# A convolution front end on one Trainium2 core: the first batch's first convolution, one tile tap by tap and two tiles of output triples

## Chip, core and metric

The kernel runs on one core of a Trainium2 chip. The metric is the device time of one execution in microseconds (us). Three runs of the kernel before the change took 255.84, 256.33 and 256.61 us; the median is 256.33 us.

The core has five engines that work side by side and wait for each other through semaphores: TensorE (in the profile PE for its matmuls and PEld for its weight loads), VectorE (DVE), ScalarE (ACT), GpSimd (POOL) and SyncE (SP), which here issues all DMA transfers. Matmul results go to PSUM, eight banks of 512 float32 columns in each of 128 partitions.

## The reference

Two batches, 4,000 samples, 512 channels, 5 taps, 8 label steps, all in bfloat16:

```python
xp = jnp.pad(x, ((0,0),(pad,pad),(0,0)))
for i in range(K):
    h = h + jnp.einsum("btc,cd->btd", xp[:, i:i+T, :], w1[i])
h = _gelu(h)[:, ::2, :]            # 2,000 samples
# the same again with w2: f = _gelu(...)[:, ::2, :], 1,000 samples
fe = jnp.einsum("btd,de->bte", f, w_f)
ge = jnp.einsum("bud,de->bue", g, w_g)
j = jnp.tanh(fe[:, :, None, :] + ge[:, None, :, :])
return jnp.einsum("btud,dv->btuv", j, w_o)
```

Only every second output of a convolution is kept, so each is computed with stride 2. The output has 2 x 1000 x 8 x 512 values, 16 MB.

## The kernel before

**Layout.** Channels lie on the partitions, 4 slices of 128 of them (index k for inputs, m for outputs). Samples lie along the free dimension, split into phases: a buffer `xs[i]` holds phases 0 to 3 of x (sample 4j + phase at column j), a buffer `xp[i]` holds phases 0 to 5 (sample 6j + phase). One column j of `xs` gives a pair of outputs of the first convolution, one column of `xp` gives a triple.

**First convolution, first batch.** Its 1,002 pairs are three tiles (`tiles`): two of 252 columns out of `xs[0]` and one of 498 out of `xs[1]`. A pair is computed by filter products: seven matmul groups (named a0, a1, a2, a3, b1, b2, b3 in `xf`, `shift` and `weight`) in place of the ten that two outputs of five taps need. Each group is four matmuls (one for each k). They need sums and differences of phases, which VectorE (`xf`) and ScalarE (`shift`) write to `xt` or in place, and sums of taps, written to `w1_t` by `w1sums` and `w1sum13`. After the matmuls `post` or `unit` adds the parts, and a gelu on ScalarE writes `hT[0]`. In the first tile, output slice m = 0 is computed tap by tap (`direct`): ten groups of four matmuls of 252 columns, with five for each output of the pair; m = 1 to 3 use the filter products.

**Second batch and second convolution.** The second batch's first convolution (out of `xp[2]`, then `xp[0]`) and both batches' second convolution (out of `hT`) run as four `Triple` tiles of 334 columns. A triple takes nine products (t0, t1, t2, tm, ti, s0, s1, sm, si) where three outputs of five taps need fifteen. Its operands are written by `Triple.step` into a work buffer `row[0]` or `row[1]` or in place. Its tap sums come from `w1part` (into `w1_x`, `w1_t`, and in place) and `w2part`. One output slice of a tile is a `Unit` with the parts s1 to s5: s1 has the product t2 and a copy of it on ScalarE, s2 tm and sm, s3 t1 and s1 and two sums on VectorE, s4 t0 and s0, s5 ti and si; three gelus write the outputs. A loop over the units interleaves s1, s3, s5, s2, s4 of neighbouring units, and puts other work (transforms of the next tile, tap sums, loads) at numbered slots (`when`, `steps`).

**The start.** The first 256 columns of `xs[0]` come by two plain loads `xr` of 128 partitions with 4 samples each (`load_xr`, 512 KB a load), transposed on TensorE and copied from PSUM by VectorE (phases 0 and 2) and ScalarE (phases 1 and 3). All other samples come by transposing DMA (`load_x` for four phases, `load_x6` for six). SP issues, in this order: two `xr`, the five taps of w1 (each after the third transfer before it has landed), eight transposes into `xs`, six into `xp[2]`; later (`load_rest`) six into `xp[0]`, four small ones, the five taps of w2 and g.

**Order.** Every operation is recorded with what it reads and writes and a cost; `schedule` then fixes an order for each engine by list scheduling: TensorE, GpSimd and SP take the first recorded operation that is ready, VectorE and ScalarE the one that is due earliest. The order is fixed when the kernel is built; the chip's engines follow it and wait where something is late. Operations recorded while `pl.pin` is true keep the recorded order; it is set to False in the first convolution.

**The rest.** Products with w_f and w_g, tanh on ScalarE, and the last product with w_o (`Plain` tiles and tiles of seven products, `Seven`) follow to the end of the span. Their code is not changed, apart from places of scratch buffers.

Lines in the profile are lines of the kernel before; most operations are recorded in helpers: 412 memset, 415 tensor_tensor, 420 activation, 428 matmul, 447 a weight load, 452 `xr`, 460 and 467 transposing loads, 503 the transposes on TensorE, 510 their copies, 577 scalar_tensor_tensor.

The functions as they stand before the change:

Of the kernel before, what the change touches and what calls it, by code (L numbers as in the profile page):

```python
# [7 lines left out]
ACT = mybir.ActivationFunctionType  # L8
# [59 lines left out]
class Plan:  # L68
# [88 lines left out]
    def schedule(self, pred):  # L157
# [19 lines left out]
        free = {e: 0.0 for e in ("pe", "act", "dve", "pool", "sp")}  # L177
# [124 lines left out]
def bass_standalone__seq2seq_rnn_t_joint__speech_kernel(  # L302
# [25 lines left out]
    NA, NB = 252, 504  # L328
# [8 lines left out]
    WHOLE = 4  # L337

    with ExitStack() as es:
# [23 lines left out]
        c_off = cur[0]  # L363
        cs = [at(f"cs{i}", [NT], FP32) for i in range(2)]
        ty = [at(f"ty{i}", [2, 256], FP32) for i in range(3)]
        s_off = cur[0]
        ws = [at(f"ws{i}", [NK, P * (2 if i == 2 else 1)], FP32) for i in range(3)]
        ssum = [at(f"ssum{i}", [NK, P], FP32) for i in range(2)]
# [6 lines left out]
        sd = [Buf(nc, f"sd{i}", [3, 336], FP32, o) for i, o in enumerate((c_off, c_off + 4096, s_off + 4096))]  # L375
        assert sd[1].end <= ty[2].end and sd[2].end <= ws[2].end
        xp = {i: Buf(nc, f"xp{i}", [6, NK, 352], BF16, xs[i].end - xs[i].bytes) for i in (0, 2)}
        assert all(xp[i].end <= xs[i].end for i in xp)
        w1_x = Buf(nc, "w1_x", [3, NK, D], BF16, wf_sb.end - wf_sb.bytes)
# [15 lines left out]
        homes = [xt_off + 8192 + i * 2048 for i in range(4)] + [v.end - v.bytes for v in ssum + ws[:2]]  # L395
# [48 lines left out]
        memset(xs[1][:, :, NT:NT + 3])  # L444
# [3 lines left out]

        def load_xr(rt):
            dst = xr[rt][:].map(lambda a: a.rearrange("p r k c -> p (r k c)"))  # L450
            src = x[0, 4 * P * rt:4 * P * (rt + 1), :].rearrange("(p r) c -> p (r c)", r=4)
            return pl.dma("sp", lambda e: e.dma_start(dst.ap, src), (), (dst,))

        def load_x(s, ph, lo, hi):

            b, half = s // 2, s % 2
            i0 = half * NB + lo - 16
            dst = xs[s % 3][ph, :, lo:hi]
            src = x[b, 4 * i0 + ph:4 * (i0 + hi - lo - 1) + ph + 1:4, :]
            pl.dma("sp", lambda e: e.dma_start_transpose(out=dst.ap, in_=src), (), (dst,), nbytes=(hi - lo) * 2 * D, rate=185e3)  # L460

        def load_x6(i, b, ph, j0, col):

            r0 = b * T + 6 * j0 + ph
            dst = xp[i][ph, :, col:col + 336]
            src = x.rearrange("b t d -> (b t) d")[r0:r0 + 6 * 335 + 1:6, :]
            pl.dma("sp", lambda e: e.dma_start_transpose(out=dst.ap, in_=src), (), (dst,), nbytes=336 * 2 * D, rate=185e3)
# [4 lines left out]
        def load_w1(i, after=None):  # L472
            o = load_w("sp", w1_sb[i], w1[i].rearrange("(k c) d -> c k d", c=P))
            if after is not None:
                o.after.append(after.idx)
            return o

        came.append(load_w1(0))
        for i in (1, 3, 4, 2):
            came.append(load_w1(i, came[-3]))  # L480
        for ph in (2, 3, 1, 0):
            load_x(0, ph, 272, 528)
        for ph in (2, 3, 1, 0):
            load_x(1, ph, 0, 512)
        for ph in (4, 0, 2, 1, 3, 5):
            load_x6(2, 1, ph, 0, 16)

        def warm_mm(n):
            o, z, zz = ps.cols(3 * NT, NT), zero[0:P], zero[:]
            for _ in range(n):  # L490
                mm(o, [(z, zz)], True, True)

        warm_mm(NWARM)
        psb = ps.h[:, :].bitcast(BF16)
        for pp in range(2):
            for rt in range(2):
                bk = 4 + 2 * pp + rt
                pv = View(psb[:, bk * 1024:(bk + 1) * 1024].rearrange("p (r k c) -> p r k c", r=2, k=NK), np.array([bk]), True)

                def fn(e, rt=rt, pp=pp, pv=pv):  # L500
                    for r in range(2):
                        for k in range(NK):
                            ins = e.transpose(pv.ap[:, r, k, :], xr[rt].h[:, 2 * r + pp, k, :], ident.h[:, :])
                    return ins
                pl.op("pe", fn, (xr[rt][:], ident[:]), (pv,), 0.8)
                o = xs[0][pp::2, :, 16 + rt * P:16 + (rt + 1) * P]
                if pp:
# [3 lines left out]


        def shift(src, off, dst, c0, n, which):

            r, d, kind = {"a0": (2, -1, 0), "a3": (0, 1, 2), "b1": (3, -1, 3)}[which]
            act(dst[kind, :, c0:c0 + n], src[r, :, off + d:off + d + n], ACT.Copy)

        def xf(src, off, dst, c0, n, which, keep=False):


            ph = lambda r: src[r, :, off:off + n]
            o = lambda kind: dst[kind, :, c0:c0 + n]
            h = NT // 2
            if which == "a0" and keep:
                tt("dve", o(0), src[2, :, off - 1:off - 1 + n], ph(2), sub)
            elif which == "b3" and keep:
                tt("dve", dst[0, :, h:h + n], ph(3), ph(1), sub)
            elif which == "a2" and keep:
                tt("dve", dst[1, :, h:h + n], ph(2), ph(0), sub)
            elif which == "a0":  # L530
                tt("dve", o(0), o(0), ph(2), sub)
            elif which == "a3":
                tt("dve", o(2), o(2), ph(0), sub)
            elif which == "b1":
                tt("dve", o(3), o(3), ph(1), sub)
            elif which == "b3":
                tt("dve", ph(3), ph(3), ph(1), sub)
            elif which == "a1":
                tt("dve", o(1), ph(0), ph(2), add)
            elif which == "a2":  # L540
                tt("dve", ph(2), ph(2), ph(0), sub)

        def operand(src, off, dst, c0, n, which, k, keep=False):
            if keep and which in ("b3", "a2"):
                return dst[("b3", "a2").index(which), k, NT // 2:NT // 2 + n]
            if which in ("a0", "a1", "a3", "b1"):
                return dst[{"a0": 0, "a1": 1, "a3": 2, "b1": 3}[which], k, c0:c0 + n]
            r = {"b3": 3, "b2": 1, "a2": 2}[which]
            return src[r, k, off:off + n]

        def weight(which, k, m):
            sl = slice(m * P, (m + 1) * P)
            taps = {"a0": 0, "b1": 1, "b3": 3, "a3": 4}
            if which in taps:
                return w1_sb[taps[which], k, sl]
            return w1_t[{"a2": 0, "b2": 1, "a1": 2}[which], k, sl]

        def w1sum13():
            v = w1_t[1]
            tt("dve", v, w1_sb[1], w1_sb[3], add)  # L560
            act(v, v, ACT.Copy, scale=2.0)

        def w1sums(m, part):


            nm = 2 if m == 2 else 1
            sl = slice(m * P, (m + nm) * P)
            s = ws[m][:]
            if part == "s":
                tt("dve", s, w1_sb[0, :, sl], w1_sb[4, :, sl], add)  # L570
            elif part == "+":
                tt("dve", w1_t[2, :, sl], s, w1_sb[2, :, sl], add)
            else:
                tt("dve", w1_t[0, :, sl], s, w1_sb[2, :, sl], sub)
# [6 lines left out]
        def w2part(m, part):  # L581
            sl = slice(m * P, (m + 1) * P)
            w = lambda i: w2_sb[i, :, sl]
            t, v, u = ssum[0][:], ssum[1][:], ws[0][:]
# [12 lines left out]

        def w1part(m, part):
            sl = slice(m * P, (m + 1) * P)
            w = lambda i: w1_sb[i, :, sl]  # L600
            pl.hold = calm
            v, u = ssum[0][:], ssum[1][:]
            if part == "s":
                s = ws[m][:] if m < 2 else ws[2][:, (m - 2) * P:(m - 1) * P]
                tt("dve", v, s, w(2), sub)
# [3 lines left out]
                act(w1_x[1, :, sl], u, ACT.Copy, scale=1.0 / 3.0)  # L609
                tt("dve", w(2), w(1), w(3), add)  # L610
                tt("dve", w1_x[2, :, sl], w(1), w(3), sub)
            else:
                act(w(1), w(1), ACT.Copy, scale=2.0)
            pl.hold = []

        banks = list(range(8))
        ends = []

        def finish(keep=0):
            while len(ends) > keep:  # L620
                ends.pop(0)()

        class Tile_:
            def __init__(self, b, src, dst, c0, i0, n, keep=False):
                self.b, self.i0, self.n, self.keep = b, i0, n, keep
# [710 lines left out]
```

## Time and profile before

| | us |
|---|---|
| median of three runs (255.84 to 256.61) | 256.33 |
| the profiled execution, its own time | 256.88 |
| its span, first to last instruction | 255.1 |
| TensorE busy | 248.3 (97%) |
| VectorE busy | 221.4 (87%) |
| ScalarE busy | 209.3 (82%) |
| GpSimd busy | 106.4 (42%) |

The profile is of one execution. Busy time is the time in which an engine had at least one instruction in work. Matmuls are pipelined and their ends are modelled, so a length of 0.27 us for one of them is not its cost; the distance between starts is. The granted TensorE clock was 1.00 of full speed from the start to 230 us and 0.99 after it. In the lists a row has the start in us, the length in us, the engine, the line, the operation, output<-inputs with buffer numbers left out, the shape, and how many instructions were merged into the row. Rows of waits have the waiting engine and what it waited for, then the total in us, how often, and the longest.

### The profile page before, as it was taken

The numbers are of one execution on the slowest core, as the hardware profiler recorded it, in microseconds if no ns is written. First come the engines' busy times: TensorE is split into PE (matmuls) and PEld (weight loads), VectorE is DVE, ScalarE is ACT, GpSimd is POOL, SyncE is SP. The second block draws the span as 40 slices with busy tenths as digits, with TensorE's granted clock in tenths as the row PEclk, the third lists the DMA queues.
The fourth block names the chain that finished last, engine by engine and source line by source line (L and its number), as shares of the span: only waits on it lengthen the run. The fifth ranks groups of instructions, "written<-read, shape, count | busy, mean of one in ns | idle before, by whom it ended". The sixth has DMA issues, their size and how long they took to land.

```text
span 255.1 us, 5158 instructions
## 1 busy us (share of the span) xinstructions
PE 248.3 (97%) x1898; PEld 182.1 (71%) x1898; DVE 221.4 (87%) x359; ACT 209.3 (82%) x333; POOL 106.4 (42%) x108
## 2 busy tenths in 40 slices
PE   8899999998999999999999999999999999999995
PEld 3899954444666666667557888877778888778873
DVE  0999799999999999993346888899899999999892
ACT  2666695769997867985499999999999999998663
POOL 1000000000000000000708899698998999689940
PEclk9999999999999999999999999999999999999999
DMA  6999999979000016000001322423254436644548
GB/s 230 312 180 212 165 187 208 164 149 335 4 0 0 3 37 211 3 0 3 1 0 42 125 82 85 137 86 110 84 166 147 137 101 197 206 142 150 178 151 269
DMA packets 56006, 31.87 MB, mean 125 GB/s; under 512 B 32926, under 2 KB 55726, under 8 KB 55982
## 3 DMA queue, kind: packets, MB, share of 16 engines
q1 hardware_dynamic: 55982, 31.55, 46.2%
q8 instruction: 15, 0.25, 0.4%
q14 instruction: 9, 0.07, 0.1%
HBM read 7.87 MB, written 16.38 MB: 95 GB/s over the span
## 4 chain that ended last, share of the span: by engine, by line
PE 71%; DVE 11%; SPq 6%; DMA 6%; issue 3%; ACT 1%; ACTq 0%; DVEq 0%
PE acc L428 71%; SPq L460 6%; DMA xs<-in_x_dram 3%; DMA w_sb<-in_w_dram 2%; DVE acc L577 2%; DVE ssum L577 2%; DVE row L415 2%; DMA xr<-in_x_dram 1%; DVE xp L415 1%; DVE xt L415 1%; DVE ty L415 1%; ACT sn L1061 1%; DVE ty L577 1%; DVE ssum L415 1%; DVE og L415 0%
## 5 line engine op out<-in xcount | busy, mean ns | idle before, releaser
L415 DVE TENSOR_TENSOR og<-acc,sn 128x512 bf16<-128x512 f32 x87 | 56.9, 681 | 4.0 <-PE acc L428 3.1
L420 ACT ACTIVATE jT<-feT,geT 128x1000 bf16<-128x1000 f32 (+6 forms) x56 | 51.7, 974 | 0.5 <-DVE feT L945 0.4
L428 PE MATMUL acc<-tw,ss 128*128 128x256 f16 x348 | 48.0, 273 | 0.0
L1124 POOL TENSOR_TENSOR ss<-jT 128x512 f16<-128x512 bf16 x28 | 33.8, 1219 | 12.9 <-ACT jT L420 10.2
L428 PEld LDWEIGHTS acc<-tw,ss 128*128 128x128 f16 x348 | 33.5, 98 | 7.3 <-DVE sn L1062 0.3
L1061 ACT ACTIVATE sn<-acc 128x512 f32<-128x512 f32 x52 | 31.4, 618 | 3.5 <-PE acc L428 2.9
L412 POOL MEMSET hT<- 128x8 bf16 (+2 forms) x6 | 0.7, 146 | 75.8 <-ACT hT L420 70.4
L428 PE MATMUL acc<-wo_sb,jT 128*128 128x256 bf16 (+1 forms) x192 | 31.7, 290 | 0.0
L428 PE MATMUL acc<-row,w_sb 128*128 128x334 bf16 x160 | 29.0, 305 | 1.2 <-DVE acc L577 1.2
L420 ACT ACTIVATE jX<-feT,geT 128x1000 bf16<-128x1000 f32 (+4 forms) x28 | 25.0, 931 | 0.0
L428 PE MATMUL acc<-xt,w_sb 128*128 128x252 bf16 (+1 forms) x144 | 23.0, 305 | 0.0
L428 PEld LDWEIGHTS acc<-wo_sb,jT 128*128 128x128 bf16 x192 | 18.8, 98 | 5.7
L1124 POOL TENSOR_TENSOR ss<-jX 128x512 f16<-128x512 bf16 x18 | 20.8, 1174 | 1.2 <-ACT jX L420 0.7
L428 PEld LDWEIGHTS acc<-row,w_sb 128*128 128x128 bf16 x160 | 15.4, 97 | 8.0 <-DVE acc L577 1.5
L1062 DVE COPY sn<-acc 128x512 f32<-128x512 f32 x25 | 16.9, 682 | 2.4 <-PE acc L428 2.3
L428 PEld LDWEIGHTS acc<-xt,w_sb 128*128 128x128 bf16 x144 | 14.1, 98 | 6.0
L428 PE MATMUL acc<-wo_sb,ss 128*128 128x256 bf16 x116 | 17.9, 273 | 0.0
L428 PE MATMUL acc<-hT,w_t 128*128 128x334 bf16 x96 | 17.6, 305 | 0.0
L428 PE MATMUL acc<-xp,w_sb 128*128 128x334 bf16 x96 | 17.2, 304 | 0.0
L1124 POOL TENSOR_TENSOR ss<-ss,jT 128x512 f16<-128x512 f16 x14 | 16.5, 1182 | 0.7 <-PE acc L428 0.4
L1124 POOL TENSOR_TENSOR ss<-jT,ss 128x512 f16<-128x512 bf16 x14 | 16.6, 1188 | 0.3
L420 ACT ACTIVATE xt<-xs 128x1008 bf16<-128x1008 bf16 (+1 forms) x8 | 10.6, 1351 | 7.1 <-DMA xs<-in_x_dram 7.1
(109 smaller groups left out, 535.6 us busy)
## 6 DMA issues: line engine op xcount, KB each, us to landing
out_dram<-og SPq DMA_DIRECT2D x44, 256.0 KB, 2.3
w_sb<-in_w_dram SPq DMA_DIRECT2D x10, 512.0 KB, 5.4
out_dram<-og SPq DMA_DIRECT2D x14, 128.0 KB, 2.7
xr<-in_x_dram SPq DMA_DIRECT2D x2, 512.0 KB, 3.8
out_dram<-ost SPq DMA_DIRECT2D x7, 128.0 KB, 2.0
wf_sb<-in_w_f_dram SPq DMA_DIRECT2D x1, 512.0 KB, 3.8
wg_sb<-in_w_g_dram SPq DMA_DIRECT2D x1, 512.0 KB, 4.9
wo_sb<-in_w_o_dram SPq DMA_DIRECT2D x1, 512.0 KB, 5.9
```

Source lines behind the costliest of these rows:

```text
L412: pl.op("pool", lambda e: e.memset(v.ap, 0.0), (), (v,))
L415: pl.op(eng, lambda e: e.tensor_tensor(out=o.ap, in0=a.ap, in1=b.ap, op=op), (a, b), (o,), 0.02 + 2.14e-3 * o.ap.free_size() if eng == "po ...
L420: pl.op("act", lambda e: e.activation(o.ap, i.ap, func, scale=scale, bias=0.0 if bias is None else bias.ap), rd, (o,), o.ap.free_size() * ...
L428: ins = e.matmul(o.ap, lhsT=l.ap, rhs=r.ap, start=start and n == 0, stop=stop and n == len(pairs) - 1, skip_group_check=not check)
L460: pl.dma("sp", lambda e: e.dma_start_transpose(out=dst.ap, in_=src), (), (dst,), nbytes=(hi - lo) * 2 * D, rate=185e3)
L577: pl.op(eng, lambda e: e.scalar_tensor_tensor(out=o.ap, in0=a.ap, scalar=f, in1=b.ap, op0=ALU.mult, op1=add), (a, b), (o,), vec_cost(o, (a ...
L1061: pl.flex({"act": (lambda e: e.activation(o.ap, v.ap, ACT.Copy), 0.05 + n * 0.833e-3), "dve": (lambda e: e.tensor_copy(out=o.ap, in_=v.ap) ...
L1062: "dve": (lambda e: e.tensor_copy(out=o.ap, in_=v.ap), 0.065 + n * 1.04e-3)}, (v,), (o,))
L1124: fn = lambda e, o=S[i], x=x, y=y, op=op: e.tensor_tensor(out=o.ap, in0=x.ap, in1=y.ap, op=op)
```

## The change

The first batch's first convolution is cut differently:

- The first tile has 216 pairs (`NA`) and is computed tap by tap for all four output slices. Both outputs of a pair go through one matmul of 432 columns: `both` makes one operand out of two stretches of 216 columns, a fixed step apart. The order is tap 0, 4, 2, 1, 3, and for each tap all four m. Banks 0 to 3 hold the results, and one gelu for each m reads them.
- The other pairs are two `Triple` tiles of 262 columns (`N3`), out of new six-phase buffers: `xq[0]` in the place of `xs[1]`, `xq[1]` in the place of `w2_sb`. The classes and helpers of the filter products (`Tile_`, `xf`, `shift`, `operand`, `weight`, `w1sums`, `w1sum13`) are gone.
- All tap sums of w1 come from `w1part`, which no longer writes w1 in place.
- `Triple` has a number of columns of its own, keeps sm and ti in other rows, and its steps are split finer (d0 to d2, r0 to r2).
- There are 24 units in place of 16, and the slots move. PSUM banks 0 to 2 are kept for second accumulators (`later`) until the second convolution's last unit.
- The second `xr` load has 90 partitions. The load order changes; the five taps of w2 move from `load_rest` to a new `load_w2` at slot 9 (after the second triple tile).
- The planner's DMA rate and start offsets change.

```diff
-    def dma(self, eng, fn, reads=(), writes=(), sem=None, nbytes=524288, rate=345e3):
+    def dma(self, eng, fn, reads=(), writes=(), sem=None, nbytes=524288, rate=320e3):
-        free = {e: 0.0 for e in ("pe", "act", "dve", "pool", "sp")}
+        free = {e: 0.75 for e in ("pe", "act", "dve", "pool", "sp")}
-    NA, NB = 252, 504
+    NA, N3 = 216, 262
...
+        xq = [Buf(nc, f"xq{i}", [6, NK, 288], BF16, v.end - v.bytes) for i, v in enumerate((xs[1], w2_sb))]
...
+        NR = (P, NA + 2 - P)
...
+        def load_xq(i, ph):
+            load_x6(xq[i], 0, ph, 2 * NA // 3 + i * N3 - 2, 0, -(-(N3 + 3 - i) // 16) * 16)
+        for kind, i in (('w', 0), ('w', 4), ('w', 2), ('w', 1), ('w', 3), ('x', 4), ('x', 0), ('x', 2), ('x', 1), ('x', 3), ('x', 5)):
...
+        for ph in (4, 0, 2, 1, 3, 5):
+            load_xq(1, ph)
...
-                if pp:
+                if rt:
                     act(o, pv, ACT.Copy)
...
             if part == "s":
+                t, v, u = ssum[4][:], ssum[m % 2][:], ssum[2 + m % 2][:]
+                if m in w13:
+                    n = slice(m * P, w13[m] * P)
+                    act(w1_t[1, :, n], w1_sb[1, :, n], ACT.Copy, scale=2.0)
+                    tt("dve", w1_t[0, :, n], w1_sb[1, :, n], w1_sb[3, :, n], add)
+                    tt("dve", w1_x[2, :, n], w1_sb[1, :, n], w1_sb[3, :, n], sub)
+                tt("dve", t, w(0), w(4), add)
                 stt("dve", u, w(4), 4.0, w(0))
                 stt("dve", u, w(2), 2.0, u)
+                act(w1_x[1, :, sl], u, ACT.Copy, scale=1.0 / 3.0)
+                tt("dve", v, t, w(2), sub)
                 act(w1_x[0, :, sl], v, ACT.Copy, scale=1.0 / 3.0)
+                tt("dve", w1_t[2, :, sl], t, w(2), add)
...
+        banks, later = [4, 5, 6, 7, 3], [0, 1, 2]
...
+        trip = [Triple(xq[0], 2, row[0], wa, to_h(0, j3, N3), N3), Triple(xq[1], 2, row[1], wa, to_h(0, j3 + N3 // 2, N3), N3),
+                Triple(xp[2], 16, row[0], wa, to_h(1, 0)), Triple(xp[0], 4, row[1], wa, to_h(1, NT3 // 2)),
...
+        memset(xq[1][0:4, :, 1 + N3:4 + N3])
+        memset(xq[1][4:6, :, N3:4 + N3])
+        taps = (0, 4, 2, 1, 3)
+        def both(i, k):
+            a, b = (xs[0][r, k, 16 + d:16 + d + NA] for r, d in tap_at[i])
+            lo, hi = a.ap, b.ap
+            ap = bass.AP(tensor=lo.tensor, offset=lo.offset, ap=[list(lo.ap[0]), [hi.offset - lo.offset, 2], [1, NA]])
+            return View(ap, np.union1d(a.cells, b.cells), False)
+        def direct(i, m):
+            mm(ps.cols(m * NT, 2 * NA), [(w1_sb[i, k, m * P:(m + 1) * P], both(i, k)) for k in range(NK)],
+               i == taps[0], i == taps[-1])
+        for i in taps:
+            for m in range(NK):
+                direct(i, m)
...
-        STEPS = ("2d", "r", "t2", "t1", "prev", "s1", "tm", "si", "sm", "next", "t0", "s0", "ti")
+        STEPS = ("d2", "d1", "d0", "r2", "r1", "t2", "tm", "sm", "r0", "t1", "s1", "prev", "s0", "next", "t0", "ti", "si")
...
+        w1part(0, "s")
+        for w in STEPS:
+            trip[0].step(w)
+        for m in range(1, NK):
+            when((0, 0, 1)[m - 1], lambda m=m: w1part(m, "s"))
+        when(17, load_late, lambda: tail_zero(1))
+        for i in range(1, len(trip) - 1):
+            steps(4 * i - 4 + 1, i, 0, 3)
+            steps(4 * i - 4 + 1, i, 3, 6)
+            steps(4 * i - 4 + 2, i, 6, 9)
+            steps(4 * i - 4 + 3, i, 9, 17)
+        when(0, load_rest)
+        when(9, load_w2)
...
-        nu = 13
+        nu = 21
```

More of the change, by code (lines that the diff above doesn't have):

```diff
@@ L362, in bass_standalone__seq2seq_rnn_t_joint__speech_kernel @@
         assert hT[0].end <= h_off + 16384 and xr[1].end <= cur[0]
[L363 to L368, printed above, removed]
+        sd = [at(f"sd{i}", [3, 336], FP32) for i in range(3)]
+        ssum = [at(f"ssum{i}", [NK, P], FP32) for i in range(5)]
         geT = at("geT", [NK * BU], FP32)
@@ L394, in bass_standalone__seq2seq_rnn_t_joint__speech_kernel @@
         assert fT[0].end <= xt_off and ost[-1].end <= h_off + hT[0].bytes
-        homes = [xt_off + 8192 + i * 2048 for i in range(4)] + [v.end - v.bytes for v in ssum + ws[:2]]
+        homes = [xt_off + 8192 + i * 2048 for i in range(4)] + [v.end - v.bytes for v in ssum[:4]]
         sn = [at(f"sn{i}", [NT], FP32, o) for i, o in enumerate(homes)]
@@ L454, in load_x @@
[L454 to L462, printed above, removed]
+            n = NR[rt]
+            dst = xr[rt].rows(0, n).map(lambda a: a.rearrange("p r k c -> p (r k c)"))
@@ L469, in bass_standalone__seq2seq_rnn_t_joint__speech_kernel, with load_w1 @@
         came = [load_xr(rt) for rt in range(2)]
         act(warm[0:1], warm[1:2], ACT.Gelu_apprx_tanh)
-        def load_w1(i, after=None):
+        def load_w1(i):
             o = load_w("sp", w1_sb[i], w1[i].rearrange("(k c) d -> c k d", c=P))
[L474 to L482, printed above, removed]
@@ L483, in bass_standalone__seq2seq_rnn_t_joint__speech_kernel @@
-        for ph in (2, 3, 1, 0):
-            load_x(1, ph, 0, 512)
+            if len(came) > 2:
+                o.after.append(came[-3].idx)
+            came.append(o)
+        def load_xq(i, ph):
+            load_x6(xq[i], 0, ph, 2 * NA // 3 + i * N3 - 2, 0, -(-(N3 + 3 - i) // 16) * 16)
+        for kind, i in (('w', 0), ('w', 4), ('w', 2), ('w', 1), ('w', 3), ('x', 4), ('x', 0), ('x', 2), ('x', 1), ('x', 3), ('x', 5)):
+            if kind == "w":
+                load_w1(i)
+            else:
+                load_xq(0, i)
@@ L543, in operand @@
[L543 to L556, printed above, removed]
@@ L727, in step @@
+                if which[0] == "d":
+                    i = int(which[1])
+                    act(r(i, n=E), z(2 * i - 2, 0, E) if i else z(4, -1, E), ACT.Copy, scale=2.0)
+                elif which[0] == "r":
+                    i = int(which[1])
+                    tt("dve", r(i, n=E), r(i, n=E), z(2 * i, 0, E), sub)
                 elif which == "next":
-                    act(r(3), r(0, 1), ACT.Copy)
+                    act(z(3), r(0, 1), ACT.Copy)
                 elif which == "prev":
@@ L988, in tail_zero @@
             memset(v)
-        tile = tiles[2]
-        calm = [pl.ops[-1].idx]
-        for m in range(NK):
-            vec = [[lambda: trip[0].step("2d"), lambda: w1part(0, "s")],
-                   [lambda: trip[0].step("r"), lambda: trip[0].step("t2"), lambda: trip[0].step("prev"),
-                    lambda: trip[0].step("t1"), lambda: w1part(1, "s")],
-                   [lambda: trip[0].step("s1"), lambda: trip[0].step("tm"), lambda: trip[0].step("si"),
-                    lambda: trip[0].step("sm"), lambda: w1part(0, "d"), lambda: w1part(2, "s")],
-                   [lambda: trip[0].step("next"), lambda: trip[0].step("t0"), lambda: trip[0].step("s0"),
-                    lambda: trip[0].step("ti"), lambda: w1part(1, "d"), lambda: w1part(3, "s")]][m]
-            tile.unit(m, vec)
-            if m == 0:
-                load_rest()
+        joint = []
         units = [Unit(t, m) for t in trip for m in range(NK)]
-        STEPS = ("2d", "r", "t2", "t1", "prev", "s1", "tm", "si", "sm", "next", "t0", "s0", "ti")
+        STEPS = ("d2", "d1", "d0", "r2", "r1", "t2", "tm", "sm", "r0", "t1", "s1", "prev", "s0", "next", "t0", "ti", "si")
         fixed = {}
```

322 lines of the change are left out of this document (57 added, 265 removed).

## The prediction, made before the changed kernel was run

> **What bounds the kernel now.** I read first the busy shares and the slices, then who TensorE waited for, then its rows and its timeline in the first 64 us.
>
> ```profile
> PE 248.3 (97%) x1898; PEld 182.1 (71%) x1898; DVE 221.4 (87%) x359; ACT 209.3 (82%) x333; POOL 106.4 (42%) x108
> ...
> DVE  0999799999999999993346888899899999999892
> ```
>
> TensorE works 248.3 of 255.1 us, and VectorE is full until about 109 us. Who TensorE waited for:
>
> ```profile
> PE acc L428 <- DVE zero L435: 1.2, 1, 1.2
> PE acc L428 <- DVE acc L577: 1.2, 1, 1.2
> PE acc L428 <- DVE xs L510: 0.7, 1, 0.7
> PE acc L428 <- DVE og L415: 0.4, 1, 0.4
> PE acc L428 <- DVE w_x L415: 0.3, 1, 0.3
> ```
>
> Only 3.8 us, all but 0.4 before 63.3 us; from there to 251 us TensorE is dense. So time gained on TensorE in the first convolution should reach the end nearly one for one, and a new wait there costs as much. The page's busy times per group overlap; what a matmul costs is read from the starts of groups that follow each other (columns: start, length, engine, line, operation):
>
> ```profile
> 32.56 0.59 PE L428 MATMUL acc<-xs,w_t 128*128 128x252 bf16 x4
> 32.99 0.59 PE L428 MATMUL acc<-xt,w_sb 128*128 128x252 bf16 x4
> 33.42 1.00 PE L428 MATMUL acc<-xs,w_t 128*128 128x498 bf16 x4
> 34.26 1.00 PE L428 MATMUL acc<-xt,w_t 128*128 128x498 bf16 x4
> ```
>
> Four of 252 columns take 0.43 us, four of 498 take 0.84: columns at 2.4 per ns plus 2.5 ns, 107.5 and 210 ns each.
>
> **TensorE's own work.** Removed from the first batch: the first tile has 40 matmuls tap by tap and 84 in filter products, the second 112, all of 252 columns; the third 112 of 498. 236 x 0.1075 + 112 x 0.210 = 48.89 us. Added: 5 taps x 4 slices x 4 outputs = 80 matmuls of 432 columns (182.5 ns by the same slope), and 2 tiles x 9 products x 16 = 288 of 262 columns (111.7 ns): 14.60 + 32.16 = 46.76. That saves 2.13 us. The 432 columns lie in two stretches of one operand, which no row shows; the nearest has three stretches:
>
> ```profile
> 123.24 1.01 PE L428 MATMUL acc<-fT,wf_sb 128*128 128x501 bf16 x4
> ```
>
> Its three starts cover 1.01 less one length of 0.376, 211 ns each, as 501 plain columns would: I take no penalty; 4 ns each, the most I can read into these digits, would be 0.3 us.
>
> A rule speaks against the exchange of many narrow matmuls for fewer wide and more narrow ones. The Trainium skill ("TensorE: Matmul & The Clock Gate", section Back-to-back issue gap) gives for streams of weight load and matmul 81 ns at 128 columns and 131 ns at 512, so that width is cheap and the count of matmuls matters. An estimate between its two figures is 37.3 us before and 38.0 after, a loss of 0.7. The trace does not agree: 498 columns take 210 ns, where that estimate has 129.
>
> **The start.** The first convolution matmul starts at 8.04 us, and the wait is put down to VectorE; the load of tap 0 is what came last:
>
> ```profile
> 1.65 0.43 SPq L447 DMA_DIRECT2D w_sb<-in_w_dram  x1
> ...
> w_sb<-in_w_dram SPq DMA_DIRECT2D x1, 512.0 KB, 6.3
> ```
>
> 1.65 + 6.3 = 7.95. The shorter sample block takes 152 KB (38 of 128 rows) from ahead of it, at the 312 GB/s of that slice 0.5 us. The copies of phases 0 and 2 now run on two engines at once (VectorE 6.1 to 6.75, ScalarE about 6.5 to 7.3) and stay ahead. I take a start at 7.55 and a gain of 0.45; bounds 0 and 0.5. Tap 4, loaded second, then lands at 9.43 - 0.45 = 9.0.
>
> **Stalls that go.** The 0.3 and the 1.17 us at 55 and 62 us are first triple products waiting for a VectorE busy without a gap. In the new kernel VectorE loses, from the first batch, 18 tile transforms, the old weight sums and all combining after the tiles: by starts some 47 us before; after it 24 weight sums (14.4), 24 transforms (14.6), the sums of 8 units (5.4) and copies (1.4), some 36. By the second batch it has lead, so I count 1.47 us gained there. What is late next lies earlier: the new hand-over.
>
> **The hand-over to triples.** The tap-by-tap tile needs only samples and taps, ends at 7.55 + 14.60 = 22.15 and covers the preparation. Two things must be ready then.
>
> First the samples, issued on SP behind the weights. Four 256-row transposes took from issue to landing:
>
> ```profile
> xs<-in_x_dram SPq DMA_TRANSPOSE x1, 7.2
> xs<-in_x_dram SPq DMA_TRANSPOSE x1, 6.4
> xs<-in_x_dram SPq DMA_TRANSPOSE x1, 4.8
> xs<-in_x_dram SPq DMA_TRANSPOSE x1, 3.9
> ```
>
> With their issues at 9.86, 11.51, 14.56 and 16.81 they landed at 17.1, 17.9, 19.4 and 20.7, later rows at about 5.3 ns each (8 landed 3,072 rows by 31.95). With 272 rows each, 0.45 us earlier, the phases 4, 0, 2, 1, 3, 5 land near 16.7, 17.7, 19.2, 20.5, 22.0, 23.4. The first product wants phase 2 doubled on ScalarE (1.04 us for 1008 columns, row xt<-xs) and two VectorE steps: 19.2 + 1.1 + 0.1 + 2 x 0.61 + 0.1 = 21.7, just under 22.15. The second tile's set ends near 32.5; its edge memsets on GpSimd wait for whole phase groups, and the double, subtract, subtract behind the last makes its first operand ready near 35, when it is due at 34.7 and some 3.5 us of the first tile's products can still go first.
>
> Second, VectorE. Its cost, too, is from starts:
>
> ```profile
> 55.80 0.68 DVE L415 TENSOR_TENSOR ssum<-ws,w_sb 128x512 f32<-128x512 f32 x1
> 56.40 0.42 DVE L415 TENSOR_TENSOR w_sb<-w_sb 128x512 bf16<-128x512 bf16 x1
> ```
>
> 0.60 us per weight sum (its full length is 0.68); likewise 0.61 for a 1048-column transform and 0.34 for a 262-column sum. Per output group `w1part` has 5 sums, per two groups 2 more: 24 x 0.60 = 14.4 us, startable from 9.0. The critical point, by due order, is the third product of the second triple tile, product 34 of a dense row at 4 x 0.1117 = 0.447 each, so 22.15 + 34 x 0.447 = 37.35. By then VectorE owes 14.4 + 12 transforms (7.3) + three units' two sums (2.0) + five transforms (3.05) = 26.8 us: ready at 9.0 + 26.8 = 35.8, with 2% for gaps 36.3, a slack of 1.0. At product 24 (32.9 us) it owes 22.5, slack 0.9. With full lengths (0.684, 0.70, 0.42) it owes 30.8 and is 2.5 late. ScalarE owes some 15 us between 20.3 and 38 and follows. So new stalls lie between 0 and 2.5, plus about 0.5 of samples; I take 0.6, because the overlapped starts are what the trace shows in a full VectorE.
>
> **Moves that cost nothing.** The second triple tile sits where conv-2 weights go, so their five loads follow unit 7, near 55 us (before: issued at 53.8), and are needed 40 us later. `load_rest` waits for the tap tile instead of the second tile; its ten loads and the earlier twelve need SP until about 54, and are wanted from 75 us. If either slipped, 20 us and more of TensorE work cover it. In `Triple.step` the operands sm and ti move to rows of the work buffer, without a change in count.
>
> **The sum.** 0.45 + 2.13 + 1.47 - 0.6 = 3.45 us. The profiled execution took 256.88 us (span 255.1 and 1.78 around it), so 253.4 for such a one; it lies 0.55 above the median 256.33, and against the median I forecast 252.9. About 0.3% (0.8 us) is what a measurement of this kernel can tell from no change.
>
> **Rivals.**
> A. Gain cut at the hand-over. VectorE pays its full lengths, or the transposes go at the slowest pace seen (4.0 us for 512 rows, 7.9 ns a row; phase 2 then lands 2.1 us later). Stalls of 2 to 3: 4.05 - 2.5 leaves 1.5, 254.8. For it: VectorE's slack is 1 us of 27. Against: 0.60 us starts throughout 40 to 62 us. Chance 0.23.
> B. Slower: VectorE becomes the bound from 22 to 45 us. Its order is fixed beforehand; if a sum that needs the last tap stands early, the sums start when that lands, near 14.2 instead of 9.0. 5.2 us late less 1.0 slack is a 4.2 us stall, which eats the 4.05; with full lengths 7.7 and 260. It decides from 4.05 us of new stalls. Against: four of the five sums of a group need taps 0, 4, 2 alone, which come first. Middle of it 258.2. Chance 0.08.
> C. Matmuls cost by count, not by width. There are 368 for 348; 20 more at the mean of 48.89 / 348 = 0.14 us lose 2.8, and 0.45 + 1.47 - 2.8 - 0.6 is 1.5 slower, 257.8. The 252 and 498 column rows, twice apart, speak against. (It is the skill's rule above, taken to its end.) Chance 0.02.
> D. The end hides it: ScalarE is busy 99.5 of the 100 us from 130 to 230, so an earlier convolution might not help, 256.3. Against: its tanh work waits for the convolutions, it is idle for a quarter before 130, and TensorE is dense beside it. Chance 0.06.
>
> **How the numbers follow.** Forecast 0.61, on its own 252.0 to 254.0 (stalls 0 to 1.5, start 0 to 0.5, the spread of the runs). A reaches to 255.4. The range 251.7 to 255.8 leaves out B, C and D, 0.16, and a thin lower end. Faster: forecast and A, 0.84. Same: D, 0.06. Slower: B and C, 0.10.
>
> **What would show it.** Right: the first 432-column matmul near 7.6, starts 182 ns apart, the 80th done near 22.2; a TensorE wait under 1 us there; the 334-column triples dense from about 55; no wait at 55 to 63. A is shown by TensorE waits of 2 to 3 us put down to VectorE or xq transposes between 22 and 40, B by more than 4 us of them. Wrong altogether would be waits above 1 us after 63 us, or 432 columns far from 182 ns.

## The result, and the profile after

The changed kernel takes 253.16 us (median of four runs, 253.08 to 253.20), the kernel before in the same comparison 256.32 us. The ratio is 0.9878 with a 95% interval of 0.9861 to 0.9895: faster by 3.2 us (1.2%). The profiled execution of the changed kernel took 253.12 us with a span of 251.3 us, against 256.88 and 255.1, so the profiled pair differs by 3.76.

The busy line and VectorE's slices, from the page after:

```profile
PE 245.3 (98%) x1914; PEld 183.6 (73%) x1918; DVE 211.6 (84%) x346; ACT 210.5 (84%) x353; POOL 106.6 (42%) x109
...
DVE  1699999966999998981546798999899999999892
```

VectorE has lost 9.8 us of busy time. It is still at nine tenths from about 13 to 50 us, but the two slices from 50 to 63 us, where the old waits were, are now at six tenths. Lines are those of the changed kernel: 410 is a tensor_tensor, 415 an activation, 423 a matmul, 496 and 503 the first samples' transposes and copies, 506 a scalar_tensor_tensor. What TensorE waited for, after (engine, line, what it waited for: us in total, times, longest):

```profile
PE acc L423 <- DVE zero L430: 1.2, 1, 1.2
PE acc L423 <- DVE xs L503: 0.5, 1, 0.5
PE acc L423 <- DVE xq L410: 0.4, 1, 0.4
PE acc L423 <- DVE og L410: 0.3, 1, 0.3
PE acc L496 <- DMA xr<-in_x_dram: 0.3, 1, 0.3
```

The 1.2 us on `acc` and the 0.3 us on `w_x` at 55 to 63 us are gone. One new wait, on `xq`, stands at the hand-over from the tap-by-tap tile to the triples. TensorE's timeline there:

```profile
7.62 14.80 PE L423 MATMUL acc<-xs,w_sb 128*128 128x432 bf16 x80 [0.51 <-DVE xs L503]
22.83 1.51 PE L423 MATMUL acc<-xq,w_x 128*128 128x262 bf16 x12 [0.41 <-DVE xq L410]
```

Eighty matmuls of 432 columns run from 7.62 without a gap; the last of them starts at 22.08. For an exact account I took the distance from each TensorE start to the next and subtracted what the first of the two costs (its columns at 2.4 per ns, plus 2.5 ns); what is left is called a loss here. A loss is given with the 0.01 us that the matmul right behind it loses too. From the first convolution matmul to the first one on g (the end of the convolutions), the work itself fell from 110.66 to 108.53 us and the losses from 1.87 (0.47 at 55.2 and 1.34 at 63.3 us) to 0.68 (0.58 of it at 22.8). The first matmul on g starts at 116.84 instead of 120.57: 3.73 us earlier, of which 0.42 is the start, 2.13 the columns, 1.18 the losses. The last matmul starts at 248.02 instead of 251.78, so all of it arrives at the end.

### The profile page after: what moved, and what is told of

Read it like the earlier page. It is cut to its first block, busy times and chain, and to the rows that moved or that the text cites. A ratio compares the mean times of both kernels' runs of the same rounds, so it can differ in the third digit from the quotient of the medians.

```text
span 251.3 us, 5192 instructions
## 1 busy us (share of the span) xinstructions
PE 245.3 (98%) x1914; PEld 183.6 (73%) x1918; DVE 211.6 (84%) x346; ACT 210.5 (84%) x353; POOL 106.6 (42%) x109
## 4 chain that ended last, share of the span: by engine, by line
PE 87%; DMA 6%; DVE 2%; ACT 1%; SPq 1%; issue 1%; ACTq 0%; DVEq 0%
PE acc L423 87%; DMA xq<-in_x_dram 2%; DMA w_sb<-in_w_dram 2%; DMA xr<-in_x_dram 1%; SPq L456 1%; DVE row L410 1%; ACT sn L838 1%; DVE ssum L410 0%; DVE og L410 0%; ACT jT L415 0%; ACT ost L838 0%; DVE xq L410 0%; DVE sn L839 0%; ACTq L338 0%; ACT og L838 0%
## 5 line engine op out<-in xcount | busy, mean ns | idle before, releaser
L423 PE MATMUL acc<-row,w_sb 128*128 128x334 bf16 (+1 forms) x224 | 39.0, 296 | 0.0
L423 PEld LDWEIGHTS acc<-row,w_sb 128*128 128x128 bf16 x224 | 21.7, 98 | 7.7
L415 ACT ACTIVATE sd<-acc 128x334 f32<-128x334 f32 (+1 forms) x48 | 20.5, 433 | 3.8 <-PE acc L423 3.2
L423 PE MATMUL acc<-row,w_t 128*128 128x334 bf16 (+1 forms) x128 | 21.1, 297 | 0.0
L506 DVE SCALAR_TENSOR_TENSOR acc<-acc,sd 128x334 f32<-128x334 f32 (+1 forms) x24 | 11.8, 491 | 10.3 <-PE acc L423 10.3
L415 ACT ACTIVATE hT<-acc 128x262 bf16<-128x262 f32 (+2 forms) x36 | 15.1, 432 | 6.2 <-PE acc L423 6.0
L423 PE MATMUL acc<-row,w_x 128*128 128x262 bf16 (+1 forms) x128 | 18.7, 290 | 0.0
```

The costliest lines, as they stand in the source:

```text
L415: pl.op("act", lambda e: e.activation(o.ap, i.ap, func, scale=scale, bias=0.0 if bias is None else bias.ap), rd, (o,), o.ap.free_size() * ...
L423: ins = e.matmul(o.ap, lhsT=l.ap, rhs=r.ap, start=start and n == 0, stop=stop and n == len(pairs) - 1, skip_group_check=not check)
L506: pl.op(eng, lambda e: e.scalar_tensor_tensor(out=o.ap, in0=a.ap, scalar=f, in1=b.ap, op0=ALU.mult, op1=add), (a, b), (o,), vec_cost(o, (a ...
```

## Experiments

Every time below is a median, every ratio is to the kernel before on the same chip. The runs went over three chips, so two of them are compared by their ratios. The change run again beside some of them gives the yardstick:

> The changed kernel itself, on the same chip as the three runs beside it, so that they have it as their measure. Both theories: as before, 3.2 to 3.8 us under the kernel before, tap tile from 7.6 us, one wait near 0.6 us (start to start) before the first triple.

Measured: 253.32 us, ratio 0.9885 (0.9858 to 0.9911). Its first tap starts at 7.67, the hand-over's loss is 0.31 instead of 0.58, the first matmul on g starts at 116.61. By the ratio it is 2.9 us (2.3 to 3.6) faster than the kernel before, a little less than the 3.2 to 3.8 expected. The hand-over differs by 0.3 us between these two executions of the same program.

**The shorter sample block undone.**

```diff
-        NR = (P, NA + 2 - P)
+        NR = (P, P)
```

> The second sample block is loaded whole again (128 partitions, 512 KB), all else as in the changed kernel. Theory (tap 0 waits behind the sample block on the DMA queues, and the first matmul waits for tap 0): tap 0 lands 0.45 us later, first 432-column matmul near 8.05 instead of 7.62, time 253.16 + 0.4 = 253.6. Rival (the start is set by the copies out of PSUM, the load is hidden): under 0.1 us, 253.2.

Measured: 253.43 us, 0.9909 (0.9874 to 0.9943), not to be told from the change. In its profile the taps start at 8.04, 0.42 later than in the change's profile, which looks like the predicted gain. The later runs take that back: over the four profiles with a whole block (before, this one and two below) the first tap starts at 8.04, 8.04, 7.55 and 7.42, mean 7.76; over eight with the block of 90 rows and 216 pairs it starts at 7.40 to 8.06, mean 7.76. The start varies by over 0.6 us between executions with the same block, and no gain of the shorter block can be seen in it. Two things lie behind it. The load of the first tap landed at 7.59 us in the mean of the four and at 7.45 in the mean of the eight, 0.14 earlier where 0.5 was expected. And with the code of the kernel before the first matmul starts 0.09 us behind that landing (two profiles), with the changed code 0.25 behind it (eight of the ten others), or later still: there two more waits on semaphores stand in between in TensorE's queue.

**Each pair of outputs in two matmuls of 216 columns instead of one of 432.**

```diff
-            mm(ps.cols(m * NT, 2 * NA), [(w1_sb[i, k, m * P:(m + 1) * P], both(i, k)) for k in range(NK)],
-               i == taps[0], i == taps[-1])
+            for s in range(2):
+                r, d = tap_at[i][s]
+                mm(ps.cols(m * NT + NA * s, NA),
+                   [(w1_sb[i, k, m * P:(m + 1) * P], xs[0][r, k, 16 + d:16 + d + NA]) for k in range(NK)],
+                   i == taps[0] and s == 0, i == taps[-1], False)
```

> Each 432-column matmul of the tap-by-tap tile becomes two of 216 columns with the same weights, 80 matmuls more. Theory (cost by width, 2.5 ns for each matmul): 160 x 92.5 ns = 14.80 us against 14.60, time +0.2, 253.4; starts 92 ns apart. Rival (cost by count, 0.14 us for each matmul): +11 us, 264.

Measured: 255.8 us, 0.9998 (0.9973 to 1.0023). The tile itself is only 0.3 us longer (first to last start 14.75 against 14.45), but the losses between 23 and 31 us grew to 0.92, 0.79, 0.25 and 0.22. The planner had costed the shorter groups differently and wrote another order, so this run mixed two things. With the cost set so that the order is that of the change:

> As the run with two matmuls of 216 columns, but with the planner told the true cost, so that the order of the work behind the tap tile is that of the changed kernel. Theory (cost by width plus 2.5 ns a matmul): 0.2 us longer tap tile, 0.2 us slower than the changed kernel on this chip. Rival (cost by count): +11 us. The excess of the earlier run, 2.3 us behind at the end of the convolutions, is then due to the other order alone.

Measured: 254.04 us, 0.9902 (0.9867 to 0.9937). TensorE's timeline of this run:

```profile
7.95 15.01 PE L423 MATMUL acc<-xs,w_sb 128*128 128x216 bf16 x160
23.86 1.40 PE L423 MATMUL acc<-xq,w_x 128*128 128x262 bf16 x11 [0.89 <-DVE xq L410]
```

160 matmuls take about what 80 took, 93 ns apart (14.76 us from first to last start): 80 more matmuls cost 0.3 us. Rival C, cost by count, would have put 80 x 0.14 = 11 us here. One matmul for both outputs is therefore worth about 0.3 us. The difference from the change between the medians, 0.7 us, lies within the intervals; in this profile it is mostly two losses of 1.07 and 0.39 us at 23.9 and 45.3 us, which are not the tile's own. The order that the planner writes can be worth more than the tile: up to the first matmul on g the other order lost 2.37 us, this one 1.59.

**Another order of taps, so that VectorE's sums start late.**

```diff
-        taps = (0, 4, 2, 1, 3)
+        taps = (0, 1, 3, 4, 2)
```

The loads change alike.

> Taps are loaded and used in the order 0, 1, 3, 4, 2 again. Then the six difference and sum steps of taps 1 and 3 can start at 10.5 us, but those with taps 4 and 2 only at 12.8 and 14.3, so VectorE's preparation starts in effect 1.5 us later. Theory (VectorE has about 1 us of lead over TensorE's triples): waits of 0.3 to 1.5 us more, +0.8, 254.0. Rival B of the prediction in full (VectorE is the bound as soon as the order is worse): +4, 257. Rival with ample lead: 0, 253.2.

Measured: 254.35 us, 0.9938 (0.9913 to 0.9963). TensorE's two longest waits behind the start:

```profile
PE acc L423 <- DVE xq L410: 0.9, 1, 0.9
PE acc L423 <- DVE og L410: 0.4, 1, 0.4
```

VectorE's sums start at 11.14 us, where they start at 8.97 in the change. The losses between 23 and 40 us are 1.9 us (1.10 at the hand-over and five smaller) against 0.62. The order of the taps, with the order of the work that the planner writes for it, matters by 1.3 us.

**The first transform ahead of the sums.** The new wait has VectorE as its releaser. Its timeline in the change:

```profile
20.85 0.70 DVE L410 TENSOR_TENSOR row<-row,xq 128x1056 bf16<-128x1056 bf16 x1
21.47 0.69 DVE L410 TENSOR_TENSOR w_x<-w_sb 128x1024 bf16<-128x1024 bf16 x1
22.07 0.70 DVE L410 TENSOR_TENSOR xq<-xq 128x1048 bf16<-128x1048 bf16 x1
```

The operand of the first triple product (`xq<-xq`) could have followed `row<-row,xq`, but a tap sum (`w_x`) stands between: 0.60 us. In this run most tap sums of output groups 2 and 3 are held back until that transform is done (`first_t2` is the transform):

```diff
+                    pl.hold = first_t2 if m > 1 else []
...
+                pl.hold = first_t2 if m > 2 else []
                 tt("dve", t, w(0), w(4), add)
                 stt("dve", u, w(4), 4.0, w(0))
+                pl.hold = first_t2 if m > 1 else []
...
+                pl.hold = []
...
+            if w == "t2":
+                first_t2 = [pl.ops[-1].idx]
```

> Tap sums of output groups 2 and 3 are held until the first triple tile's first operand (t2) is written, which in the changed kernel waited behind two of them on VectorE. Theory (TensorE's wait of 0.6 us from start to start at the hand-over is VectorE's order, not the samples): the wait goes, -0.5, 252.65. Rival (VectorE is short of time, so the wait moves to later products): 253.2 with waits of about 0.5 us between 23 and 40 us.

Measured: 253.65 us, 0.9912 (0.9879 to 0.9944). The triples now start at 22.35, right behind the taps, and the wait is gone. In its place come losses of 0.21, 0.24, 0.34, 0.09 and 0.08 us between 23 and 34 us, 0.96 in all against 0.62. The rival came true: the wait moved, and this order gains nothing. It fits that VectorE is short of time in the whole stretch: in the change's profile it has no idle time above 0.05 us from 17.1 to 34.0 us.

**More work for VectorE in that stretch.**

```diff
-                tt("dve", t, w(0), w(4), add)
+                for _ in range(3):
+                    tt("dve", t, w(0), w(4), add)
```

> In each of the four groups the weight sum t = w0 + w4 is written three times instead of once (the same values): 8 more sums of 1024 columns on VectorE, 8 x about 0.6 us = +4.8 us of its time between about 14 and 35 us. Theory (VectorE leads the products by only about 1 us, as the 1.9 us of waits in the run with the other tap order suggest): TensorE waits 3 to 4 us more between 22 and 45 us for w_x or xq, and the time is 256.2 to 257.2. Rival (VectorE has lead to spare in this stretch, and the hand-over's wait comes from a late load alone): no more waits than in the change, 253.2.

Measured: 257.32 us, 1.0065 (1.0038 to 1.0093), slower than the kernel before and a little above the expected range. TensorE's waits in that stretch:

```profile
PE acc L423 <- DVE xq L410: 0.8, 1, 0.8
PE acc L423 <- DVE sd L410: 0.7, 2, 0.5
...
PE acc L423 <- ACT sd L415: 0.6, 2, 0.5
```

By starts the losses between 22 and 48 us are 0.99, 0.11, 0.33, 0.50, 0.65, 0.46, 0.66, 0.35, 0.37 and 0.13: 4.55 against 0.62. Of 4.8 us added, 3.9 reached TensorE in this profile, so VectorE's lead was about 0.9 us. It is the profile of the fastest of twelve runs (256.11); by the ratios the run is 4.6 us behind the change, with about 1 us of uncertainty, so the lead is small but not known to a tenth. At 55 to 63 us there is still no wait.

**Longer tap-by-tap tiles.** 222 pairs and triples of 260:

```diff
-    NA, N3 = 216, 262
+    NA, N3 = 222, 260
```

> Tap tile of 222 pairs, triples of 260 columns. Theory (the tap tile is cover for samples and VectorE): columns +0.16 us, second block 6 rows longer +0.1 at the start, tile ends 0.5 us later, so that the 0.6 us wait shrinks to 0.1: 0.25 us faster than the changed kernel. Rival (the wait is made by VectorE's order and goes along with the end of the tile): 0.26 us slower.

Measured: 253.03 us, 0.9878 (0.9840 to 0.9916), the same as the change. The hand-over's loss is 0.40, with 0.15 and 0.14 later; the first matmul on g starts at 117.26. The wait did not shrink to the 0.1 us of the theory, and a quarter of a microsecond either way is less than this run can tell. Then 240 pairs and triples of 254, whose second sample block has 114 rows (`NA, N3 = 240, 254`):

> Tap tile of 240 pairs, triples of 254 columns. Theory: columns +0.64 us, start +0.3, wait 0.6 gone: 0.3 us slower than the changed kernel. Rival (the wait goes along with the end of the tile): 0.95 us slower. Rival (VectorE's lead limits far beyond the hand-over): faster than the changed kernel.

Measured: 256.37 us, 1.0007 (0.9986 to 1.0027): the whole gain lost, and not where the sizes would have it. TensorE's timeline, and then windows of it (us, PE busy and count, the other engines, granted clock, DMA share, GB/s):

```profile
5.36 0.61 PE L496 MATMUL acc<-ident,xr 128*128 128x128 bf16 x8
8.21 2.16 PE L496 MATMUL acc<-ident,xr 114*128 114x114 bf16 x24 [2.25 <-DMA xr<-in_x_dram]
10.16 2.14 PE L423 MATMUL acc<-xs,w_sb 128*128 128x480 bf16 x5
```

```profile
5.00:8.00 3.00, 0.97 (x10) 0.58 (x8) 0.69 (x1) 0.00 (x0) 0.00 (x0) 1.00 0.97 250
8.00:10.00 2.00, 1.79 (x23) 1.79 (x24) 0.35 (x1) 0.93 (x1) 0.00 (x0) 0.67 0.76 242
10.00:12.00 2.00, 2.00 (x9) 0.92 (x8) 1.55 (x3) 0.93 (x1) 0.14 (x1) 0.50 0.94 323
12.00:27.00 15.00, 15.00 (x75) 7.19 (x74) 15.00 (x26) 9.65 (x14) 0.00 (x0) 1.00 1.07 214
```

The block of 114 rows landed at about 8.2 us; blocks of 90, 96 and 128 rows land at 5.3 to 5.8. TensorE stood idle for 2.25 us, and after that the mean granted clock was 0.67 and then 0.50 until 12 us, which cost the first five matmuls of 480 columns 1 us more. (In finer windows it is 1.00 until 8.6 us, 0.50 from 8.8 to 12.0 and 1.00 again from 12.3.) The same size with the block loaded whole (`NR = (P, P)`):

> The tile by taps is 240 columns per output half instead of 216 (matmuls of 480 columns) and the triples 254 instead of 262, with the second block of samples loaded whole (128 rows instead of the 114 that the run with 240 columns loaded). Theory (that run's loss was the late landing of its 114-row block and the low clock behind the idle time): the block lands near 5.4 us, the taps start near 8.05, the granted clock stays 1.0, and the cost is columns +0.64, start +0.4, hand-over wait -0.3 to -0.6: 253.7. Rival (240 columns cost 3 us by themselves): 256.4.

Measured: 253.75 us, 0.9924 (0.9896 to 0.9952), the forecast number, though not by its terms: the taps started at 7.42 instead of 8.05, and losses of 0.25 and 0.42 came at 28 and 30 us though the hand-over's own went. So 240 columns do not cost 3 us; the load of 114 rows did. The Trainium skill ("DMA: Bandwidth & Descriptors", section Why a DMA increments its semaphore by 16 and not by 1) says that a transfer is split over the largest number of DMA engines up to 16 that divides the slowest dimension of both its sides. By that, 128 and 96 rows get 16, 90 rows get 15 and 114 rows get 6; the landings agree, and no run here counts the engines.

**The old stalls.** To see whether the waits at 55 and 63 us were a VectorE with too much to do, two of its sums were taken from the kernel before:

```diff
-        for w in ("a2", "b1", "b3", "a3"):
+        for w in ("b1", "a3"):
```

> The kernel before, with two of the third tile's transforms (b3 and a2) left out: their buffers keep what an earlier tile left there, so the outputs of the third tile are other numbers. Two VectorE sums of about 1.1 us fall away just ahead of the two waits of 0.47 and 1.34 us that TensorE shows at 55 and 63 us. Theory (these waits are VectorE's queue running late, and the change removes them by asking less of it): both waits go, -1.8 us, 254.5. Rival (the waits end on something else, as a load or ScalarE's evictions): they stay, 256.3.

Measured: 255.79 us, 0.9997 (0.9970 to 1.0024). No gain: the theory fell. The wait of 0.47 went; the other, 1.34, came back as 1.51. TensorE and VectorE in this run:

```profile
62.57 0.74 PE L428 MATMUL acc<-row,w_sb 128*128 128x334 bf16 x4 [1.34 <-DVE acc L577]
```

```profile
60.57 0.41 DVE L415 TENSOR_TENSOR w_sb<-w_sb 128x512 bf16<-128x512 bf16 x1
60.91 0.41 DVE L415 TENSOR_TENSOR w_x<-w_sb 128x512 bf16<-128x512 bf16 x1
61.24 0.85 DVE L415 TENSOR_TENSOR row<-row,xp 128x1344 bf16<-128x1344 bf16 x1
62.01 0.50 DVE L577 SCALAR_TENSOR_TENSOR acc<-acc,sd 128x334 f32<-128x334 f32 x1
```

TensorE waits for the sum that reads a PSUM bank (`acc<-acc,sd`). VectorE gave up two sums (about 2.2 us), but the order written for it put five other operations (two `w_x`, one `w_sb`, one `ssum`, one `row`: 2.4 us by starts) ahead of that sum which stood behind it before. The stall is a matter of a full queue's order, not of its length alone.

**The tail.** In most profiles, before and after alike, 0.88 us is lost between 219 and 227 us (223 and 231 before), and in some it is not. VectorE in the change, and then in the run with the whole block:

```profile
215.05 2.54 DVE L901 TENSOR_TENSOR ss<-jT,ss 128x512 f16<-128x512 bf16 x1
217.51 1.87 DVE L410 TENSOR_TENSOR og<-acc,sn 128x512 bf16<-128x512 f32 x3
219.31 0.41 DVE L901 TENSOR_TENSOR ss<-ss,jX 128x512 f16<-128x512 f16 x1
```

```profile
215.79 1.45 DVE L901 TENSOR_TENSOR ss<-jT,ss 128x512 f16<-128x512 bf16 x1
217.16 1.88 DVE L410 TENSOR_TENSOR og<-acc,sn 128x512 bf16<-128x512 f32 x3
```

One and the same sum takes 2.54 to 2.57 us in nine profiles and 1.44 or 1.45 in four; the last matmul follows the first one on g by 131.17 to 131.23 us in the nine and by 130.32 to 130.34 in the four. So the sum is given to GpSimd:

```diff
-                    pl.flex({k: alt[k] for k in (("dve", "pool"))}, (x, y), (S[i],))
+                    pl.flex({k: alt[k] for k in (("pool",) if (self.n, i) == (21, 3) else ("dve", "pool"))}, (x, y), (S[i],))
```

> The change, with one sum of the last convolution's input (the one that took VectorE 2.54 us beside GpSimd's sums, in place of 0.41) given to GpSimd instead. Theory (the 0.88 us of TensorE's waits between 219 and 227 us come from these two engines slowing each other): the waits go, 252.4. Rival (another VectorE operation meets GpSimd's longer list in its place): the waits come back within 2 us of where they were, 253.2.

Measured: 252.65 us (252.29 to 252.79), 0.9874 (0.9839 to 0.9910). From the first matmul on g to the last it takes 130.68 us: the losses of 0.54 and 0.22 us are gone, and 0.13 at 224.4 and 0.21 at 236.4 us came in their place. Theory and rival are each half right. It has the lowest median of all, but its interval lies over that of the change (0.9858 to 0.9911), so that it beats the change is not shown.

## Why the prediction was right, step by step

The forecast was 252.9, the result 253.16. The sign and the size came out as argued, and so did the largest term. Of the three others, the start's gain was not there, the stalls were counted too low, and the hand-over had the forecast size at another operand than the one it was worked out for. The signs that the prediction named came: the first matmul of 432 columns at 7.62 us, the eightieth at 22.08, a wait under 1 us behind it, none at 55 to 63 and none above 1 us later.

**TensorE's own work**: 2.13 us forecast. The account above uses the same price, so its 2.13 is no second measurement; what measures it is that almost nothing is left over. Outside the losses named, the profile before has 0.05 us left up to the first matmul on g and the one after has 0.10. The matmuls of 432 columns start 183 ns apart, so the two stretches of one operand cost nothing that can be seen. This is the part that carried the result, and the price by columns is what made it: the rows of 216, 262 and 432 columns agree on it. The Trainium skill's figures ("TensorE: Matmul & The Clock Gate", section Back-to-back issue gap) would have made the exchange a loss of 0.6 (by the prediction's way of estimating, whose sum before is 37.4 us, not 37.3), and the run with two matmuls speaks against them once more: an estimate between its two figures has 92 ns at 216 columns and 121 at 432, so that two for one would cost 80 x 0.064 = 5 us, where 0.3 was measured.

**The start**: 0.45 forecast, 0.42 in the profiled pair, but nothing in the mean of twelve profiles. The step "takes 152 KB from ahead of it, 0.5 us" failed: the first tap's load landed at 7.17 to 7.95 us behind a whole block and at 7.16 to 7.82 behind the short one. The profiled execution of before was merely at the late end. Nor do the copies always "stay ahead": in the runs with another tap order and with two matmuls and the change's order, the first matmul started right behind ScalarE's copy, at 7.85 and 7.95, though the tap had landed at 7.40.

**Stalls that go**: 1.47 forecast from the idle times in the waits, 1.81 found. The term was mis-sized because an idle time leaves out what the matmul records' modelled ends cover; starts against starts show 0.47 and 1.34 where the waits show 0.30 and 1.17. That they go was right in every profile of the change and its variants. The reason given, that VectorE has lead by then, shows in VectorE's timeline around the sum that TensorE waited for, before:

```profile
62.11 0.68 DVE L415 TENSOR_TENSOR ssum<-ws,w_sb 128x512 f32<-128x512 f32 x1
62.71 0.51 DVE L577 SCALAR_TENSOR_TENSOR acc<-acc,sd 128x334 f32<-128x334 f32 x1
```

and the same sum after, the first of 334 columns:

```profile
57.74 0.51 DVE L506 SCALAR_TENSOR_TENSOR acc<-acc,sd 128x334 f32<-128x334 f32 x1 [3.05 <-PE acc L423]
```

Before, it stood in a queue without a gap; after, VectorE had been idle for 3.05 us and waited for TensorE. The run with more sums supports it too: it was late until 37 us and yet had no wait at 55 to 63. But the run with less work in the kernel before shows that two sums less do not do it, and no run separates what the change owes to more lead from what it owes to another order.

**The hand-over**: 0.6 forecast, 0.58 and 0.31 found in two executions. The samples came as worked out: phases 4, 0, 2, 1, 3, 5 landed at 15.3, 17.7, 19.1, 20.7, 22.3 and 23.6 us against 16.7, 17.7, 19.2, 20.5, 22.0 and 23.4. The step that failed is the one that had the first operand ready at 21.7, before the taps end: it was done at 22.8, because two tap sums of 0.60 us each (`ssum` at 20.25 and `w_x` at 21.47) stood between the transforms on VectorE. Where the prediction looked for the stall, near 37 us at the third product of the second triple tile, there is no loss. So the 0.6 us, chosen between 0 and 2.5, is right in size partly by luck. That VectorE is the cause, with little lead, is right: the prediction worked out a slack of 1.0 us, and the run with more sums gives about 0.9.

**The sum**: without the start, 2.13 + 1.81 - 0.62 is 3.3 us, near the 3.16 between the medians. The forecast's 3.45 came close because a start counted 0.45 too high and stalls counted 0.34 too low nearly cancel, which is luck.

**The rivals.** A (a loss of 2 to 3 us at the hand-over) needs VectorE to pay its full lengths; its starts stay 0.60 to 0.62 apart; or late samples, which came near the forecast. It is what 1.9 us of losses in the run with another tap order come close to. B (VectorE becomes the bound) is what the run with more sums shows: 4.8 us more of work turn 3.2 us of gain into a loss. By an estimate from this run, the change stands about 1 us of VectorE's work from the edge that B named, and some 4 us (0.9 of lead and the gain of 3.2) from a loss. C (cost by count) fell with the run of two matmuls. D (the end hides it) fell: of 3.73 us at the first matmul on g, 3.76 arrive at the last.

## What to carry to other kernels

Price a matmul by the distance of starts in rows of its own width, and count a stall by starts against starts. When an engine is full, an edit that takes work from it need not take away the wait behind it: look at what the new order puts ahead of the operation that is waited for. Before a gain of a few tenths is put down to an edit at the start, look at how much the start varies between executions.

## What the runs showed of the hardware

A VectorE sum of two 2-byte buffers in SBUF waits for GpSimd's. In the change all 18 `ss` sums on VectorE that took over 0.5 us (alone, 0.41) end 0.28 or 0.29 us after the end of a GpSimd `ss` sum, which takes 1.15 to 1.35 us. The sum above ended behind one GpSimd sum in four profiles and behind two in nine, though in all thirteen it began within 0.03 us of a GpSimd sum's start; what decides it is finer than the trace shows. The Trainium skill ("SBUF — State Buffer", section Who interferes with whom) says that a VectorE instruction with two SBUF inputs contends with a GpSimd instruction that reads SBUF, and calls the port pair that they share an exclusive lock. The trace agrees, and adds that the loser can lose twice in a row, which here is worth 0.87 us at the end.

In the run with 240 columns and the block of 114 rows, 2.25 us without a matmul (and only transposes just before and behind them) were followed by 3.4 us, from 8.7 to 12.1, at a granted clock of 0.50; a load that was late by 2.8 us so cost another 1 us. With the block loaded whole the clock stays at 1.00. It does not happen in every execution: nine of the twelve runs have a mean granted clock of 0.987 to 0.993 and times of 255.79 to 257.65 us, three have 0.998 or 1.000 and 255.63 to 255.97.
